# Combining a weight matrix as it is read, and reordering normalised rows for an unstrided transpose, in a scheduled attention + two-FFN kernel

## The chip, the cores and the metric

The kernel runs on one core of a Trainium2 chip. The engines named below are PE (TensorE, matrix products), PEld (its weight loads), DVE (VectorE), ACT (ScalarE), POOL (GpSimd) and SP (SyncE, whose queue issues all DMA transfers here). The metric is device time in microseconds (us) of one execution, lower is better.

## The reference

```python
# attention: two softmax attentions per head (4x downsampled, and a band of |i-j| < 4), added
out_up = np.repeat(sm_attn(q_d, k_d, v_d), factor, axis=2)
...
x = (out_up + out_local) -> (4, 576, 512)
# first feed-forward, gated
k = np.maximum(xk @ w_k, 0.0);  v = k * k @ w_v
x = v * sigmoid(xr @ w_r)
# second feed-forward
xn = (x - mu) / np.sqrt(var + 1e-06) * g_ln
ch = np.maximum(xn @ w_ch1, 0.0) @ w_ch2        # w_ch1 512 x 2048, w_ch2 2048 x 512
return x + ch
```

The weights come as float64, so a row of 512 elements is 4 KB. 2304 tokens are taken in six chunks of 384.

## The kernel before

**Products.** Every float32 factor is split in a high part (rounded to the format that PE multiplies, by a cast on ACT or DVE) and a low part (the difference, a subtraction on DVE or POOL); `mm3` (L793) makes one product of three matmuls.

**Weights.** `load_f32` (L399) reads 512 KB of float64 into a tile `w` (two of them) and makes float32 of it with two ACT operations (L411, L413) and two DVE operations (L418, L422), into a tile `wf` (two of them). `load_split` (L426) then splits it: a cast (L391 or L392) and a subtraction (L436).

**The second feed-forward** runs in three passes of two chunks each. Its first product uses a seven-product scheme of 2x2 blocks in all passes; w_ch1's seven combinations were prepared earlier (`w1_combine`) and lie in DRAM as `s_dram`, read back as tiles `sa`. In the first pass the second product is plain: `m2_h` makes the hidden values of step f (f = 0 to 7; the 16 row blocks of w_ch2 are used in pairs f and f+8), with DVE adding partial sums from PSUM (`u` L1129, `t` L1135 and L1138, `c` L1142 and L1146) and making low parts (`c11l`, `c22l`, `c12l`, `c21l`, L1115), and `m2_acc` multiplies them with the pair's high and low parts (`w20h` to `w215l`) into `pso`. In the second and third pass the second product too is made of seven, and needs w_ch2's combinations, which `w2_combine` (L1198) prepares during the first pass and writes to `t_dram`.

**`w2_combine` before.** For each pair f it puts the float32 rows together again by adding high and low part (L1215, two additions of 512 elements), then makes four differences of 256 elements in place (L907), splits each into a tile `t` (cast L391 or L392, subtraction L903) and writes the tile to DRAM (L1225). The tiles `t` live in four buffers that go by the tag `wa`; a fifth `t` must wait until the first one's write has landed. Each pair also writes copies of its parts (L1207). All eight pairs are released by `after`, a step of the first pass's products that lies three steps before the pair's own (parameter `tg`).

**Normalisation.** `m2_prep` (L972) normalises a chunk's rows (`x1t`, L1005, DVE), writes them to `z_dram` (L1008), reads them back 32 partitions at a time as `zb` (L1020), and transposes 32x32 blocks on DVE (L1026): feature 4p+kt goes to partition p, so the transpose reads every fourth element. The rows of w_ch1 and g_ln are read in the same order of features.

**Order of the work.** Nothing is issued in the order of the code. `add` collects operations with their dependences, a due time and a cost; `Plan.order` builds, for each engine, one fixed sequence, choosing between ACT, DVE and POOL where an operation has several ways; SP's queue too is one sequence. On the chip each engine works through its own sequence and waits where it must. So a late operation holds back all that stand behind it on its engine.

## Time and profile before

| | us |
|---|---|
| three runs | 766.68, 768.57, 770.2 |
| median | 768.57 |
| the profiled execution | 770.0 |
| its span in the trace | 767.9 |

The profiled execution lies 1.4 us above the median of the runs, and 2.1 us of it lie outside the traced span. Times in the rows below count from the start of the span. The first pass of the second feed-forward runs from about 388 to 523 us, the other two to 764.5 us.

### The profile page before, as it was taken

The numbers are of one execution on the slowest core, as the hardware profiler recorded it, in microseconds if no ns is written. First come the engines' busy times: TensorE is split into PE (matmuls) and PEld (weight loads), VectorE is DVE, ScalarE is ACT, GpSimd is POOL, SyncE is SP. The second block draws the span as 40 slices with busy tenths as digits, with TensorE's granted clock in tenths as the row PEclk, the third lists the DMA queues.
The fourth block names the chain that finished last, engine by engine and source line by source line (L and its number), as shares of the span: only waits on it lengthen the run. The fifth ranks groups of instructions, "written<-read, shape, count | busy, mean of one in ns | idle before, by whom it ended". The sixth has DMA issues, their size and how long they took to land.

```text
span 767.9 us, 17471 instructions
## 1 busy us (share of the span) xinstructions
PE 744.3 (97%) x6248; PEld 662.6 (86%) x6248; DVE 622.6 (81%) x1322; ACT 469.2 (61%) x1079; POOL 93.7 (12%) x143
## 2 busy tenths in 40 slices
PE   9899999999999999999999999889999999999998
PEld 6778777888778798888989888778999999999998
DVE  5889999998975958978996889698777996344986
ACT  5789998987885856858841444363346552443552
POOL 3002112212100000000010000140012112110101
PEclk9999999999999999999999999899999999999999
DMA  8998595887786996982388999789999888986684
GB/s 186 184 191 188 165 195 130 170 178 154 202 179 202 277 322 179 281 248 98 108 293 256 285 298 332 272 268 347 329 295 345 235 255 268 391 261 209 203 269 147
DMA packets 199325, 180.33 MB, mean 235 GB/s; under 512 B 92480, under 2 KB 139976, under 8 KB 199240
## 3 DMA queue, kind: packets, MB, share of 16 engines
q1 hardware_dynamic: 199240, 179.23, 80.3%
q8 instruction: 50, 0.82, 0.5%
q14 instruction: 35, 0.29, 0.1%
HBM read 134.09 MB, written 45.09 MB: 233 GB/s over the span
## 4 chain that ended last, share of the span: by engine, by line
PE 70%; DVE 12%; DMA 10%; ACT 5%; issue 3%; POOL 1%; SPq 0%; DVEq 0%; ACTq 0%; POOLq 0%
PE pso L796 6%; PE pso L794 6%; PE pso L795 6%; PE psh L794 6%; PE psh L795 6%; PE psh L796 6%; DMA w<-in_moe_w_ch_dram 4%; PE psk L794 4%; PE psv L794 4%; PE psv L795 4%; PE psv L796 4%; PE psk L796 3%; PE psk L795 3%; DMA sa<-s_dram 2%; PE sc L645 2%
## 5 line engine op out<-in xcount | busy, mean ns | idle before, releaser
L794 PE MATMUL psh<-xn,sa 128*128 128x384 f32 x336 | 114.6, 341 | 5.1 <-DVE c L1142 2.9
L795 PE MATMUL psh<-xn,sa 128*128 128x384 f32 x336 | 113.4, 337 | 0.0
L796 PE MATMUL psh<-xn,sa 128*128 128x384 f32 x336 | 113.2, 337 | 0.0
L391 ACT CAST hh<-q 128x384 fp32r<-128x384 f32 x109 | 56.2, 516 | 48.0 <-PE pso L795 43.7
L796 PE MATMUL pso<-ta,hl 128*128 128x256 f32 x300 | 84.4, 281 | 0.0
L794 PE MATMUL pso<-ta,hh 128*128 128x256 f32 x300 | 84.3, 281 | 0.0
L795 PE MATMUL pso<-ta,hh 128*128 128x256 f32 x300 | 84.3, 281 | 0.0
L794 PEld LDWEIGHTS psh<-xn,sa 128*128 128x128 f32 x336 | 63.4, 189 | 11.0 <-DVE c L1142 4.1
L795 PEld LDWEIGHTS psh<-xn,sa 128*128 128x128 f32 x336 | 63.4, 189 | 1.9
L796 PEld LDWEIGHTS psh<-xn,sa 128*128 128x128 f32 x336 | 63.4, 189 | 0.0
L903 DVE TENSOR_TENSOR hl<-q,hh 128x384 fp32r<-128x384 f32 x92 | 51.3, 564 | 9.2 <-ACT hh L391 8.5
L796 PEld LDWEIGHTS pso<-ta,hl 128*128 128x128 f32 x300 | 56.7, 189 | 0.0
L795 PEld LDWEIGHTS pso<-ta,hh 128*128 128x128 f32 x300 | 56.6, 189 | 0.0
L794 PEld LDWEIGHTS pso<-ta,hh 128*128 128x128 f32 x300 | 56.5, 188 | 0.0
L1273 ACT ACTIVATE q<-q 128x384 f32<-128x384 f32 x48 | 25.2, 525 | 45.3 <-DVE q L1263 26.3
L411 ACT ACTIVATE wf<-w 128x512 f32<-128x512 f32 x48 | 32.2, 672 | 20.3 <-DMA w<-in_moe_w_ch_dram 13.9
L418 DVE SCALAR_TENSOR_TENSOR wf<-wf,w 128x512 uint32<-128x512 uint32 x48 | 33.3, 695 | 10.5 <-ACT w L413 9.2
L903 POOL TENSOR_TENSOR hl<-q,hh 128x384 fp32r<-128x384 f32 x20 | 21.3, 1072 | 144.3 <-ACT hh L391 144.2
L395 ACT ACTIVATE kr<-psk 128x384 f32<-128x384 f32 x46 | 22.4, 487 | 26.1 <-PE psk L796 23.9
L859 DVE TENSOR_TENSOR kl<-kr,kh 128x384 fp32r<-128x384 f32 x43 | 23.8, 552 | 15.2 <-ACT kr L858 14.9
L907 DVE TENSOR_TENSOR q<-q,q 128x384 f32<-128x384 f32 x60 | 35.1, 592 | 0.0
L413 ACT ACTIVATE w<-w 128x512 uint32<-128x512 uint8 x52 | 34.8, 670 | 0.0
(593 smaller groups left out, 2109.1 us busy)
## 6 DMA issues: line engine op xcount, KB each, us to landing
sa<-s_dram SPq DMA_DIRECT2D x168, 256.0 KB, 4.9
ta<-t_dram SPq DMA_DIRECT2D x100, 256.0 KB, 3.5
w<-in_moe_w_ch_dram SPq DMA_DIRECT2D x32, 512.0 KB, 5.5
s_dram<-s SPq DMA_DIRECT2D x56, 256.0 KB, 4.0
t_dram<-t SPq DMA_DIRECT2D x32, 256.0 KB, 4.4
vw<-in_v_dram SPq DMA_DIRECT2D x62, 96.0 KB, 4.3
x_dram<-r SPq DMA_DIRECT2D x18, 256.0 KB, 2.7
x1t<-x_dram SPq DMA_DIRECT2D x6, 768.0 KB, 5.7
```

The costliest lines, as they stand in the source:

```text
L391: return [("ACT", c_act(n), lambda: nc.scalar.copy(dst(), src()), False), ("DVE", c_dve(n, True), lambda: nc.vector.tensor_copy(dst(), src ...
L395: return [("ACT", c_act(n, True), lambda: nc.scalar.activation(dst(), src(), AF.Relu), False), ("DVE", c_dve(n), lambda: nc.vector.tensor_ ...
L411: add("ACT", c_act(512), prio, lambda: nc.scalar.activation(f(), w64().bitcast(F32)[:, :, 1], AF.Abs, scale=2.0 ** -112), r=[w64], w=[f])
L413: add("ACT", c_act(512), prio, lambda: nc.scalar.activation(w64()[:, :, 0], w64().bitcast(U8).rearrange("p a (b c) -> p a b c", c=4)[:, :, ...
L418: lambda: nc.vector.scalar_tensor_tensor(fu(), fu(), 3, w64()[:, :, 0], op0=ALU.logical_shift_left, op1=ALU.bitwise_or),
L794: nc.tensor.matmul(ps, lh, rh, start=start, stop=False, skip_group_check=more)
L795: nc.tensor.matmul(ps, lh, rl, start=False, stop=False, skip_group_check=more)
L796: nc.tensor.matmul(ps, ll, rh, start=False, stop=stop, skip_group_check=more)
L859: add(either(C, lambda e: e.tensor_tensor(kl(), kr(), kh().bitcast(F32), op=ALU.subtract)), 0, prio, None, r=[kr, kh], w=[kl])
L903: add(either(n, lambda e: e.tensor_tensor(lo(), src(), hi().bitcast(F32), op=ALU.subtract)), 0, prio, None, r=r + wh, w=wl)
L907: add(either(n, lambda e: e.tensor_tensor(out(), a(), b(), op=op)), 0, prio, None, r=r, w=w)
L1273: return [("ACT", c_act(n), lambda: nc.scalar.activation(t(), t(), AF.Relu), False), ("DVE", c_dve(n, True), lambda: nc.vector.tensor_scal ...
```

## The change

Two edits, and a parameter of the planner:

1. For f = 2 to 7 the new `w2_pair` reads both row blocks of a pair, splits them, and gives the two float32 tiles to `w2_combine`, which makes its differences in them in place. The two additions (L1215 before) remain for f = 0 and 1 alone. These six pairs are no longer released by `after`; they are due ten microseconds (`tp`) after the pair's reading. Both blocks of a pair are due at the same time.
2. The normalisation (L1005 before) writes its 512 features in another order (4 x 4 x 32), so that the block for kt lies in 32 neighbouring elements and the transpose reads them unstrided. The rows of w_ch1 and g_ln are read in their natural order, 128 neighbouring rows instead of every fourth.
3. `ahead`, with which the planner lets SP's queue run ahead of its transfers, goes from 1 to 2 us.

```diff
-    late=330.0, ahead=1.0, tp=0.5, tps=0.05, keep=2, tg=-3, b11=6, ne=12, we=52.842, wes=25.704, wel=6.378,
+    late=330.0, ahead=2.0, tp=10, tp0=0.5, tps=0.05, keep=2, tg=-3, b11=6, tq=0, ne=12, we=52.842, wes=25.704, wel=6.378,
...
-    def w1_rows(d, fo):
-        return w_ch1.rearrange("(p k) f -> k p f", k=KT)[d, :, 512 * fo:512 * fo + 512]
...
-        load_f32(w1_rows(d, fo), f, prio)
+        load_f32(w_ch1[d * P:(d + 1) * P, 512 * fo:512 * fo + 512], f, prio)
...
-                    x1t()[:, TT], x1t()[:, t], mv()[:, t, 0:1], rstd()[:, t:t + 1], op0=ALU.subtract, op1=ALU.mult),
+                    x1t()[:, TT].rearrange("p (a k f) -> p k a f", k=KT, f=32),
+                    x1t()[:, t].rearrange("p (k a f) -> p k a f", k=KT, f=32),
+                    mv()[:, t, 0:1], rstd()[:, t:t + 1], op0=ALU.subtract, op1=ALU.mult),
...
-                        out=b()[:, q, C // 2 * h:C // 2 * h + C // 2], in_=zb()[:, :, kt:P:KT]),
+                        out=b()[:, q, C // 2 * h:C // 2 * h + C // 2], in_=zb()[:, :, 32 * kt:32 * kt + 32]),
...
+    def w2_pair(f, prios):
+
+        raw = []
+        for k in range(2):
+            g, prio = f + F4 * k, prios[k]
+            hi = Buf(wp, [P, 512], F32R, f"s{2 * f + k}h", 1, f"w2{g}h")
+            lo = Buf(wp, [P, 512], F32R, f"s{2 * f + k}l", 1, f"w2{g}l")
+            b = Buf(wk, [P, 512], F32, "wf", 2, "t")
+            load_f32(w_ch2[g * P:(g + 1) * P, :], b, prio)
+            split(512, hi, lo, b, prio, [b], [hi], [lo])
+            W2[g] = hi, lo
+            raw.append(b)
+        w2_combine(f, prios[1] + PRM["tp"], None, raw)
...
-        for k in range(2):
+        for k in range(0 if made else 2):
...
         for o in plan.ops[n0:]:
-            o.deps.add(after)
+            if after is not None:
+                o.deps.add(after)
...
+    if KEEP == 1:
+        for f in range(2, F4):
+            w2_pair(f, [T_2 + PRM["w2"] + PRM["w2s"] * (2 * f - 4)] * 2)
...
-            for f in range(F4):
-                w2_combine(f, T + DP * (PRM["tp"] - 1.0 + PRM["tps"] * f), acc_op[min(max(f + PRM["tg"], 0), F4 - 1)])
+            for f in range(2 if KEEP == 1 else F4):
+                w2_combine(f, T + DP * (PRM["tp0"] - 1.0 + PRM["tps"] * f), acc_op[min(max(f + PRM["tg"], 0), F4 - 1)])
```

What the planner makes of it, at three places. First DVE's sequence in step f = 5 of the first pass, where combinations stand between the partial sums. Before (`t` without a step's line L1138 is a combination; `c21l` and `u` are the step's own work):

```order
L903 TENSOR_TENSOR t<-t 128x256
L1215 TENSOR_TENSOR t<-w23h,w23l 128x512
L903 TENSOR_TENSOR t<-t 128x256
L907 TENSOR_TENSOR t<-t 128x256
L1215 TENSOR_TENSOR t<-w211h,w211l 128x512
L903 TENSOR_TENSOR t<-t 128x256
L907 TENSOR_TENSOR t<-t 128x256
L1115 SCALAR_TENSOR_TENSOR c21l<-c_6736,c21h 128x384
L1129 TENSOR_TENSOR u<-psh_6747,u 128x384
```

The same step's end in the changed kernel:

```order
L903 TENSOR_TENSOR t<-t 128x256
L1229 TENSOR_TENSOR t<-w20h,w20l 128x512
L1229 TENSOR_TENSOR t<-w28h,w28l 128x512
L907 TENSOR_TENSOR t<-t 128x256
L1114 SCALAR_TENSOR_TENSOR c12l<-c_6687,c12h 128x384
L1145 TENSOR_TENSOR c_6733<-psh_6654,u 128x384
L907 TENSOR_TENSOR t<-t 128x256
L388 COPY u<-psh_6714 128x384
L1114 SCALAR_TENSOR_TENSOR c21l<-c_6733,c21h 128x384
L903 TENSOR_TENSOR t<-t 128x256 x2
L1128 TENSOR_TENSOR u<-psh_6763,u 128x384
```

The pairs 2 to 5 are combined by then, and pair 0 follows directly on pair 6; one L903 stands ahead of `c21l` in these rows instead of three, and two now stand between `c21l` and `u`.

Second, DVE's sequence at the turn from the first feed-forward (`r` is its last output, L877) to the second. Before:

```order
L418 SCALAR_TENSOR_TENSOR wf<-wf,w_5565 128x512
L907 TENSOR_TENSOR raw_5428<-raw_5428 128x384
L422 SCALAR_TENSOR_TENSOR wf<-w_5565,wf 128x512
L877 TENSOR_TENSOR r<-psv_5388,r 128x512
L877 TENSOR_TENSOR r<-psv_5394,r 128x512
L877 TENSOR_TENSOR r<-psv_5400,r 128x512
L1129 TENSOR_TENSOR u<-psh_5663,u 128x384
L436 TENSOR_TENSOR w210l<-wf,w210h 128x512
```

In the changed kernel:

```order
L903 TENSOR_TENSOR w210l<-t,w210h 128x512
L903 TENSOR_TENSOR t<-t 128x256
L907 TENSOR_TENSOR t<-t 128x256
L1082 TENSOR_TENSOR xn<-raw_5428,xn 128x384
L907 TENSOR_TENSOR t<-t 128x256
L903 TENSOR_TENSOR t<-t 128x256
L907 TENSOR_TENSOR t<-t 128x256
L903 TENSOR_TENSOR t<-t 128x256
L877 TENSOR_TENSOR r<-psv_5388,r 128x512
L877 TENSOR_TENSOR r<-psv_5394,r 128x512
L877 TENSOR_TENSOR r<-psv_5400,r 128x512
L1128 TENSOR_TENSOR u<-psh_5662,u 128x384
```

Pair 2 is combined here, ahead of `r` and `u`; the conversion of its second block has moved further up.

Third, SP's queue at the same place (`w` are reads of w_ch2, `sa` the first product's weights of step 1). Before:

```order
L405 DMA w_5637<-in_moe_w_ch_dram 128x1024
L1094 DMA sa_5667<-s_dram 128x512
L1094 DMA sa_5677<-s_dram 128x512
L405 DMA w_5706<-in_moe_w_ch_dram 128x1024
L879 DMA x_dram<-r 128x512
L977 DMA x1t<-x_dram 128x3x512 x2
L879 DMA x_dram<-r 128x512
L1094 DMA sa_5779<-s_dram 128x512
```

In the changed kernel:

```order
L405 DMA w_5636<-in_moe_w_ch_dram 128x1024
L405 DMA w_5658<-in_moe_w_ch_dram 128x1024
L1093 DMA sa_5668<-s_dram 128x512
L1220 DMA t_dram<-w210h 128x2x256
L1093 DMA sa_5683<-s_dram 128x512
L1220 DMA t_dram<-w210l 128x2x256
L1239 DMA t_dram<-t 128x512 x3
L879 DMA x_dram<-r 128x512
L1239 DMA t_dram<-t 128x512
L1093 DMA sa_5744<-s_dram 128x512
```

The third `sa` of step 1 now stands behind the four writes of pair 2's combinations.

Counted over the kernel, DVE's sequence loses twelve additions L1215 and thirteen operations L907 on `t`, POOL's gains thirteen operations on `t` (9 before, 22 after), six copies of 256 elements (L1196) go from ACT to DVE, and PE's sequence holds the same matmuls, a few of them moved past each other in the first pass.

## Rows read from the trace of the kernel before

**Rows 1.** The page's first part: busy us (share of span) x instructions.

```profile
span 767.9 us, 17471 instructions
...
PE 744.3 (97%) x6248; PEld 662.6 (86%) x6248; DVE 622.6 (81%) x1322; ACT 469.2 (61%) x1079; POOL 93.7 (12%) x143
```

**Rows 2.** Busy time by stretch: length, then PE, PEld, DVE, ACT, POOL, granted clock, DMA.

```profile
388.00:425.00 37.00, 36.66 (x186) 33.21 (x185) 28.11 (x66) 10.70 (x24) 2.00 (x2) 1.00 0.85 274
425.00:455.00 30.00, 28.73 (x140) 24.88 (x139) 25.54 (x53) 14.95 (x28) 1.02 (x1) 1.00 0.94 301
455.00:482.00 27.00, 26.68 (x130) 22.93 (x129) 24.74 (x53) 12.77 (x27) 2.21 (x3) 1.00 0.98 322
482.00:500.00 18.00, 15.17 (x64) 13.35 (x64) 12.44 (x30) 5.67 (x14) 3.08 (x4) 0.81 0.76 267
500.00:523.00 23.00, 19.27 (x91) 15.97 (x90) 21.92 (x46) 14.87 (x40) 7.77 (x7) 1.00 0.81 271
```

**Rows 3.** PE's waits from 388 to 523: us in total, times, longest.

```profile
PE psh L794 <- DVE c L1142: 2.9, 2, 2.2
PE pso L796 <- DVE c21l L1115: 2.8, 1, 2.8
```

**Rows 4.** PE in order of time: start, us, operation, idle before it.

```profile
485.56 0.40 PE L795 MATMUL pso<-w213l,c21h 128*128 128x512 f32 x1
488.78 0.79 PE L796 MATMUL pso<-w213h,c21l 128*128 128x512 f32 x1 [2.83 <-DVE c21l L1115]
```

**Rows 5.** The stretch behind that wait, columns as in Rows 2.

```profile
488.70:494.80 6.10, 6.02 (x16) 5.07 (x17) 4.74 (x11) 1.32 (x4) 2.49 (x4) 0.50 0.63 233
```

**Rows 6.** DVE in order of time ahead of the same wait.

```profile
484.65 0.69 DVE L1215 TENSOR_TENSOR t<-w211h,w211l 128x512 f32<-128x512 f32 x1
487.50 0.43 DVE L903 TENSOR_TENSOR t<-t 128x256 fp32r<-128x256 f32 x1 [2.16 <-ACT t L391]
488.18 0.55 DVE L1115 SCALAR_TENSOR_TENSOR c21l<-c,c21h 128x384 fp32r<-128x384 f32 x1
```

**Rows 7.** ACT in order of time there.

```profile
487.06 0.41 ACT L391 CAST t<-t 128x256 fp32r<-128x256 f32 x1 [2.44 <-DMA t_dram<-t]
```

**Rows 8.** Instructions writing the tiles t, 455 to 522: ns min/median/max; DMA landing.

```profile
L907 DVE TENSOR_TENSOR t<-t x25: 411/419/1220, 462.2 to 517.4; 128x256 f32<-128x256 f32 x25
L907 POOL TENSOR_TENSOR t<-t x7: 726/736/892, 464.8 to 502.1; 128x256 f32<-128x256 f32 x7
...
DMA to landing us min/median/max: 3.6/4.4/5.1
```

**Rows 9.** The additions L1215 alone, 455 to 523: length, DVE busy (count), clock, DMA.

```profile
455.00:523.00 68.00, 11.34 (x16) 0.95 0.86 290
```

**Rows 10.** DVE's transposes, strided and unstrided, ns min/median/max.

```profile
L1026 DVE STREAM_TRANSPOSE raw<-zb x48: 473/492/541, 361.9 to 569.8; 128x192 f32<-128x192 f32 x48
...
L704 DVE STREAM_TRANSPOSE pT<-e x16: 530/570/574, 20.0 to 227.9; 128x384 f32<-128x384 f32 x16
```

**Rows 11.** The normalisation L1005, ns min/median/max.

```profile
L1005 DVE TENSOR_SCALAR x1t<-x1t,mv,rstd x18: 536/542/550, 324.9 to 554.2; 128x512 f32<-128x512 f32 x18
```

**Rows 12.** DVE operations that ran beside a POOL operation, in order of time.

```profile
492.39 1.04 DVE L1215 TENSOR_TENSOR t<-w212h,w212l 128x512 f32<-128x512 f32 x1
...
517.40 1.22 DVE L907 TENSOR_TENSOR t<-t 128x256 f32<-128x256 f32 x1
```

**Rows 13.** DVE in order of time at the turn to the second feed-forward.

```profile
387.58 2.00 DVE L877 TENSOR_TENSOR r<-psv,r 128x512 f32<-128x512 f32 x3
389.50 0.55 DVE L1129 TENSOR_TENSOR u<-psh,u 128x384 f32<-128x384 f32 x1
```

**Rows 14.** PE at the third product of step 1 (f = 1), in order of time.

```profile
400.11 0.33 PE L794 MATMUL psh<-xn,sa 128*128 128x384 f32 x1
```

**Rows 15.** The page's list of DMA issues: count, KB each, median us to landing.

```profile
sa<-s_dram SPq DMA_DIRECT2D x168, 256.0 KB, 4.9
```

**Rows 16.** PE's waits from 523 to 768: us in total, times, longest.

```profile
PE psh L794 <- DMA sa<-s_dram: 1.0, 2, 0.6
```

More of the change, by code (lines that the diff above doesn't have):

```diff
@@ L904, in split, with minus @@
             r=r + wh, w=wl)
-    def minus(n, out, a, b, prio, r, w, op=ALU.subtract):
-        add(either(n, lambda e: e.tensor_tensor(out(), a(), b(), op=op)), 0, prio, None, r=r, w=w)
+    def minus(n, out, a, b, prio, r, w, op=ALU.subtract, skip=False):
+        add(either(n, lambda e: e.tensor_tensor(out(), a(), b(), op=op))[skip:], 0, prio, None, r=r, w=w)
     n_put = [0, 0]
@@ L938, in w1_combine @@
             else:
-                load_f32(w1_rows(d, fo), a[x], prio)
+                load_f32(w_ch1[d * P:(d + 1) * P, 512 * fo:512 * fo + 512], a[x], prio)
         def put(i, src):
@@ L1196, in w2_stay, with w2_combine @@
             add(copy(256, B11[f][x], lambda x=x: W2[f][x]()[:, :256]), 0, prio, None, r=[W2[f][x]], w=[B11[f][x]])
-    def w2_combine(f, prio, after):
+    def w2_pair(f, prios):
[10 more added lines that the diff above has]
+        w2_combine(f, prios[1] + PRM["tp"], None, raw)
+    def w2_combine(f, prio, after, raw=None):
         n0 = len(plan.ops)
@@ L1210, in w2_combine @@
                     w=[(td, (i, f, x)) for i in range(i0, i0 + n)], lat=2.2)
-        raw = [Buf(wk, [P, 512], F32, "wf", 2, "t") if KEEP == 1 else
-               Buf(wk, [P, 512], F32, f"xr{HL[k]}", 1, "t") for k in range(2)]
-        for k in range(2):
+        made = raw is not None
+        raw = raw or [Buf(wk, [P, 512], F32, "wf", 2, "t") if KEEP == 1 else
+                      Buf(wk, [P, 512], F32, f"xr{HL[k]}", 1, "t") for k in range(2)]
+        for k in range(0 if made else 2):
             h_, l_ = W2[f + F4 * k]
             add(either(512, lambda e, k=k, h_=h_, l_=l_: e.tensor_tensor(
-                raw[k](), h_().bitcast(F32), l_().bitcast(F32), op=ALU.add)), 0, prio, None, r=[h_, l_],
+                raw[k](), h_().bitcast(F32), l_().bitcast(F32), op=ALU.add))[k < PRM["tq"] % 4:], 0, prio, None, r=[h_, l_],
                 w=[(raw[k], 0), (raw[k], 1)])
@@ L1220, in w2_combine @@
         for n, (o, x, y) in enumerate(((0, 1, 0), (1, 3, 1), (3, 3, 0), (2, 2, 3)), 3):
-            minus(256, s(o), s(x), s(y), prio, [rk(x), rk(y)], [rk(o)])
+            minus(256, s(o), s(x), s(y), prio, [rk(x), rk(y)], [rk(o)], skip=n - 3 < PRM["tq"] // 4 % 8)
             t = Buf(w1tiles, [P, 2, 256], F32R, "wa", 4, "t")
@@ L1408, in attn_moe_kernel @@
                     out=raw()[KT * i:KT * i + KT, :P],
-                    in_=src.rearrange("(p k) -> k p" if src is g_ln else "(k p) -> k p", p=P)), w=[(raw, i)], lat=2.2)
+                    in_=src.rearrange("(k p) -> k p", p=P)), w=[(raw, i)], lat=2.2)
             vps = Buf(ps_k, [P, 512], F32, "pk", 2, "vps")
@@ L1497, in attn_moe_kernel @@
         moe_x(c, pvs[c], rr, T + DU + 1 + PRM[f"rx{c}"])
+    if KEEP == 1:
+        for f in range(2, F4):
+            w2_pair(f, [T_2 + PRM["w2"] + PRM["w2s"] * (2 * f - 4)] * 2)
     for i, f in enumerate(w2_order[4:], 4):
-        W2[f] = load_split(w_ch2[f * P:(f + 1) * P, :], i, f"w2{f}", T_2 + PRM["w2"] + PRM["w2s"] * (i - 4))
+        if f not in W2:
+            W2[f] = load_split(w_ch2[f * P:(f + 1) * P, :], i, f"w2{f}", T_2 + PRM["w2"] + PRM["w2s"] * (i - 4))
     DP = PRM["dp"]
```

## The prediction

> **What bounds the kernel now.** I read the page first: PE is busy 744.3 of the span's 767.9 us [rows 1]. The change adds no matmul and takes none away, so it can only give back time in which PE waits or runs slowly, and what such time there is bounds the gain. The busy time by stretch shows where: over the first pass of the second feed-forward, which the change rearranges, PE is not busy for 0.34 + 1.27 + 0.32 us up to 482, and for 2.83 + 3.73 us from 482 to 523 [rows 2]. [...] The pool is 1.93 + 6.56 + 3.05 = 11.5 us, of which 9.6 lie behind 482. Behind the first pass PE's waits on named releasers come to the 1.0 us of one group [rows 16].
>
> The list of PE's waits names DVE for it: `c` L1142 and `c21l` [rows 3]. In order of time, the long one runs from 485.6 to 488.8 and ends on `c21l` [rows 4]. `c21l` had nothing late of its own: DVE stood for 2.16 us at a subtraction of a combination `t`, and the two rows behind it had to wait [rows 6]. That subtraction waited for ACT's cast, and the cast for a write to `t_dram` [rows 7]: the fifth `t` needs a buffer whose write takes 4.4 us to land [rows 8]. Right behind that wait the clock is at 0.50 [rows 5]. So the loss is a chain: combinations come faster than four buffers can be written, and DVE, in one sequence, holds the first product's sums behind them. From 500 on DVE is simply full, 21.92 of 23 us [rows 2].
>
> **The change, part by part.** *Additions removed.* Sixteen of L1215 take 11.34 us, 0.71 each [rows 9]; twelve go, 8.5 us of DVE. All the pairs stood in one stretch because `after` released them late; now six pairs are combined as they are read. Counted in the two sequences, behind `c21l` of step 5 (488 us) and its neighbours stood about five pairs of eight operations on `t` and ten L1215; now about two and a half pairs, two L1229, and pair 7's conversion (six operations of 512 elements, for which I take L1215's 0.71). With 0.42 us for an operation on `t` [rows 8], DVE's 12.44 + 21.92 = 34.4 us between 482 and 523 [rows 2] become 34.4 - 7.1 - 16.8 + 1.4 + 8.4 + 4.3 = 24.6, and with the six copies that come over from ACT (no such row; between nothing and 0.42 each, I take 0.42) 27.1. PE needs 41 - 9.6 = 31.4 us for what it does there. DVE is then no longer full, and the 3.73 us behind 500 should go. The stall at 485 needs both the crowd and the buffers; the crowd shrinks, but pair 0 follows directly on pair 6 and pair 1 on pair 7, eight `t` through four buffers each time. I keep one wait of the size seen, 2.2 us [rows 6], without a fall of the clock, as PE has more behind it. Its bounds are nothing and the whole 9.6.
>
> *POOL's share.* Thirteen operations on `t` go from DVE to POOL: DVE saves 13 x 0.42 = 5.4 us, POOL spends 13 x 0.74 = 9.6 [rows 8]. That is not free for DVE: beside a POOL operation, an addition took 1.04 instead of 0.71 and a difference 1.22 instead of 0.42 [rows 9, 12, 8], so 0.33 to 0.80 us more each, 4.3 to 10.4 us for thirteen. DVE's saving by the additions and this one together, 13.9 us, then falls to between 3.5 and 9.6. It remains a saving, in a stretch where it was full, so I leave the estimate above. [...]
>
> *The turn at 388.* Pair 2 is now combined ahead of `r` and `u`. Seven operations on `t` are 2.9 us of DVE; two conversions of 0.71 that stood there have gone further up. `r` starts at 387.58 and `u` ends at 390.05 [rows 13]; behind `u` PE waits for its bank. Bounds: nothing, if PE's last products are what `r` waits for, and 2.9. I take 1.0, under the net 1.5, as `r` does read PE's last results.
>
> *SP's queue.* The third `sa` of step 1 now stands behind pair 2's four writes. These are ready when their subtractions are, which stand ahead of `r`, so about 388 to 390; with 4.9 us to landing [rows 15] the `sa` is there at about 395, and PE wants it at 400.11 [rows 14]. Cost nothing, covered by step 0's products; without that cover it would cost up to the 4.9.
>
> *The reordered normalisation.* A transpose of 192 elements takes 492 ns strided; an unstrided one of 384 takes 570 [rows 10]. An unstrided one of 192 is not in the trace: it lies between half of 570 and the present 492, a saving of 0 to 0.21 us. I take 0.1, so 1.6 us of DVE in each pass's sixteen. L1005 writes the same 512 elements in another order; between no change and the 0.71 of L1215, that is 0 to 0.17 us on its 0.54 [rows 11, 9], for six in a pass up to 1.0. Both stand where DVE has room: it is busy 28.11 of 37 us in the stretch where the first pass has them, and PE loses 0.34 there [rows 2]. Zero in the sum, at most 1.6 either way (PE's 0.34 + 1.27). The natural order of w_ch1's and g_ln's rows moves the same bytes; PE's waits ahead of 388 name no transfer. Zero. `ahead` changes SP's sequence only, as counted.
>
> *Sum.* 9.6 - 2.2 - 1.0 = 6.4 us gained. From the profiled execution's own 770.0 that is 763.6; against the median, which lies 1.4 lower, 762.2, and I forecast **762**.
>
> **The rivals.** *The wait stays (no change).* Eight `t` in a row still meet four buffers, twice, and POOL's operations slow DVE; one of the two places pays what 482 to 495 paid, 2.83 + 3.05 = 5.9 us, while the 3.73 behind 500 goes: 3.73 - 1.0 = 2.7 gained, 765.9; were both to pay, about 768 to 770. For it: landing of 4.4 us, two times for eight tiles, is 8.8 us in a step of some 16 (388 to 523 in eight steps). Against it: reads and combinations of pairs 2 to 5 are gone from there. [...]
>
> *More than I count.* All waits of the first pass go, and the turn costs nothing: 768.6 - 11.5 = 757; with the 1.0 of the later passes, 756. For it: the early waits are DVE's as well, and DVE has less to do. Against: 425 to 455 now gets pairs 4 and 5 complete.
>
> *Slower.* The place is SP's single queue: each pair's four writes now stand between the `sa` of the next step, and a `t` that waits for its buffer holds back the `sa` behind its write. If each of the pairs 3 to 7 pays once what 482 to 495 paid, 5 x 5.9 = 29.5 us come in and 11.5 go, with 1.0 for the turn: 768.6 + 19 = 787.6. It makes the kernel measurably slower from about 3 us for each pair on ((11.5 + 3.8) / 5). For it: the DMA share is 0.94 and 0.98 from 425 to 482 already [rows 2], and the writes come earlier into that. Against it: in the first pass none of PE's waits is on an `sa`, though writes stood between them before as well.
>
> *It does not do what it says.* The transposes may be no faster; as they are hidden, the time is the forecast's.
>
> **How the numbers follow.** Forecast 0.54 (its own range 759 to 765), the wait stays 0.22, more 0.13, slower 0.11. The range reaches over the second and third case and leaves out the slower one and some of the edges: 756 to 769. The three runs lie within 3.5 us, so 0.5% (3.8 us) is about what a measurement here can tell from no change; that is 764.7 and 772.4. Faster: forecast and more, 0.67; within: 0.22; slower: 0.11.
>
> **What would show it.** Right: no L1215 for pairs 2 to 7 and DVE under about 90% between `c21l` of step 5 and the first pass's end; no wait of PE over 2.5 us there and no stretch at 0.50; `u` at the turn at most a microsecond later; transposes nearer 390 than 492 ns and L1005 near 542. Wrong: a wait of PE of 3 us or more on `c21l`, `c` or `u` with a cast on a `t_dram` write behind it (the wait stays); PE waiting on `sa` in the first pass (slower); all PE waits there under 2 us in sum (more). The forecast fails above all if waits move to the step where pair 0 follows pair 6.

## The result, and the profile after

The changed kernel takes 759.83 us (median of 6 runs, 756.88 to 764.1) against 769.68 (6 runs, 766.68 to 773.1): a ratio of 0.9868, 95% interval 0.9826 to 0.991. Run once more with its variants it came to 0.9871 (0.9842 to 0.9899). The forecast was 762 us, in a range of 756 to 769.

The busy time by stretch of the changed kernel, in the stretches of [rows 2] and in one more (length, then PE, PEld, DVE, ACT, POOL, granted clock, DMA share, GB/s):

```profile
388.00:425.00 37.00, 36.16 (x178) 31.31 (x178) 30.05 (x70) 12.53 (x29) 5.83 (x7) 1.00 0.97 336
425.00:455.00 30.00, 29.52 (x143) 25.50 (x143) 25.74 (x57) 15.13 (x30) 4.83 (x5) 1.00 0.83 256
455.00:482.00 27.00, 27.00 (x136) 24.29 (x135) 23.65 (x47) 14.17 (x31) 7.30 (x9) 1.00 1.03 360
482.00:500.00 18.00, 18.00 (x91) 16.12 (x90) 15.52 (x35) 9.44 (x24) 4.21 (x5) 1.00 0.99 347
500.00:523.00 23.00, 22.95 (x120) 21.02 (x119) 18.03 (x39) 10.39 (x25) 5.55 (x5) 1.00 0.97 340
523.00:640.00 117.00, 114.74 (x812) 113.23 (x811) 94.26 (x203) 54.00 (x113) 15.25 (x14) 1.00 0.88 272
```

The last of these stretches in the kernel before:

```profile
523.00:640.00 117.00, 116.05 (x802) 114.28 (x801) 98.50 (x209) 57.81 (x124) 16.62 (x15) 1.00 0.91 299
```

Read the difference of length and PE. From 482 to 523 PE is busy for all but 0.05 us, where 6.56 us were missing, and the clock is at 1.00 throughout, where half of the 6.10 us at 0.50 [rows 5], 3.05 us, is counted as lost: 9.56 us come back. From 388 to 482, 0.84 + 0.48 us are missing instead of 1.93: 0.61 more. From 523 to 640, 2.26 us are missing instead of 0.95: 1.31 are given back. The sum is 8.86 us; the spans are 767.9 and 759.0, 8.9 apart.

What the clock of 0.50 cost is to be seen in the starts of PE's matmuls in the kernel before, two pairs of them at 0.50 and two behind it at 1.00:

```profile
490.37 0.52 PE L794 MATMUL psh<-xn,sa 128*128 128x384 f32 x1
490.69 0.52 PE L795 MATMUL psh<-xn,sa 128*128 128x384 f32 x1
...
492.61 0.63 PE L794 MATMUL pso<-w213h,c21h 128*128 128x512 f32 x1
493.04 0.63 PE L795 MATMUL pso<-w213l,c21h 128*128 128x512 f32 x1
...
496.68 0.33 PE L794 MATMUL psh<-xn,sa 128*128 128x384 f32 x1
496.85 0.33 PE L795 MATMUL psh<-xn,sa 128*128 128x384 f32 x1
...
499.28 0.40 PE L794 MATMUL pso<-w26h,c11h 128*128 128x512 f32 x1
499.51 0.39 PE L795 MATMUL pso<-w26l,c11h 128*128 128x512 f32 x1
```

At 0.50 the next matmul starts 0.32 us (384 elements) or 0.43 us (512) later, at 1.00 0.17 or 0.23. The sixteen from 488.78 on, ten of 512 and six of 384, take 6.33 us up to the start of the next; at the spacings of 1.00 that is an estimated 3.4, so 3.0 us were lost there, beside the 3.05 counted.

PE's waits in the changed kernel, first from 388 to 523 (where the kernel before has those of [rows 3]), then from 530 to 600 (us in total, times, longest):

```profile
PE psh L794 <- DVE c L1145: 0.5, 1, 0.5
PE psh L794 <- ACT u L387: 0.3, 1, 0.3
PE pso L796 <- DVE c11l L1114: 0.2, 1, 0.2
PE psh L794 <- DVE t L1134: 0.2, 1, 0.2
...
PE psh L794 <- ACT q L1288: 1.5, 1, 1.5
PE psh L794 <- DVE q L1275: 0.6, 1, 0.6
```

None of the first pass is on `c21l` any more. The waits of the second pass are new. DVE in order of time shows where they come from: four transposes stand ahead of a sum, and wait for a read `zb`:

```profile
549.94 1.16 DVE L1025 STREAM_TRANSPOSE raw<-zb 128x192 f32<-128x192 f32 x4 [1.78 <-DMA zb<-z_dram]
551.02 0.52 DVE L1275 TENSOR_TENSOR q<-psh,u 128x384 f32<-128x384 f32 x1
...
555.44 1.16 DVE L1025 STREAM_TRANSPOSE raw<-zb 128x192 f32<-128x192 f32 x4 [1.92 <-DMA zb<-z_dram]
556.52 0.52 DVE L1284 TENSOR_TENSOR q<-psh,u 128x384 f32<-128x384 f32 x1
```

Next the operations of [rows 10, 11] and the turn of [rows 13] in the changed kernel (ns min/median/max; then start and us):

```profile
L1025 DVE STREAM_TRANSPOSE raw<-zb x48: 334/338/380, 361.9 to 560.1; 128x192 f32<-128x192 f32 x48
...
L1002 DVE TENSOR_SCALAR x1t<-x1t,mv,rstd x18: 531/541/548, 325.2 to 540.8; 128x512 f32<-128x512 f32 x18
...
387.75 1.88 DVE L877 TENSOR_TENSOR r<-psv,r 128x512 f32<-128x512 f32 x3
389.55 0.54 DVE L1128 TENSOR_TENSOR u<-psh,u 128x384 f32<-128x384 f32 x1
```

A transpose takes 338 ns instead of 492, the normalisation 541 instead of 542, and `u` ends at 390.09 instead of 390.05.

### The profile page after: what moved, and what is told of

Read it like the earlier page. It is cut to its first block, busy times and chain, and to the rows that moved or that the text cites. A ratio compares the mean times of both kernels' runs of the same rounds, so it can differ in the third digit from the quotient of the medians.

```text
span 759.0 us, 17473 instructions
## 1 busy us (share of the span) xinstructions
PE 741.1 (98%) x6248; PEld 659.9 (87%) x6248; DVE 609.6 (80%) x1304; ACT 466.5 (61%) x1073; POOL 101.2 (13%) x155
## 4 chain that ended last, share of the span: by engine, by line
PE 73%; DMA 10%; DVE 8%; ACT 6%; issue 2%; SPq 0%; POOL 0%; DVEq 0%; POOLq 0%; ACTq 0%
PE pso L796 8%; PE pso L795 8%; PE pso L794 8%; PE psh L794 6%; PE psh L795 6%; PE psh L796 6%; PE psk L794 4%; PE psk L796 3%; PE psk L795 3%; DMA zb<-z_dram 3%; PE psv L794 3%; PE psv L796 3%; PE psv L795 3%; DMA w<-in_moe_w_k_dram 2%; PE warm L449 1%
## 5 line engine op out<-in xcount | busy, mean ns | idle before, releaser
L903 DVE TENSOR_TENSOR hl<-q,hh 128x384 fp32r<-128x384 f32 x93 | 51.4, 557 | 9.6 <-ACT hh L391 8.5
L794 PEld LDWEIGHTS pso<-ta,hh 128*128 128x128 f32 x300 | 56.5, 188 | 0.0
L903 POOL TENSOR_TENSOR hl<-q,hh 128x384 fp32r<-128x384 f32 x19 | 19.8, 1047 | 152.8 <-ACT hh L391 152.7
L907 DVE TENSOR_TENSOR q<-q,q 128x384 f32<-128x384 f32 x60 | 34.2, 577 | 0.0
L411 ACT ACTIVATE wf<-w 128x512 f32<-128x512 f32 x36 | 24.2, 672 | 16.1 <-DMA w<-in_moe_w_k_dram 5.3
L818 DVE SCALAR_TENSOR_TENSOR tmu<-xT,oms,tmu 128x384 f32<-128x384 f32 (+1 forms) x64 | 31.8, 513 | 2.7 <-ACT tmu L812 2.6
```

The costliest lines, as they stand in the source:

```text
L411: add("ACT", c_act(512), prio, lambda: nc.scalar.activation(f(), w64().bitcast(F32)[:, :, 1], AF.Abs, scale=2.0 ** -112), r=[w64], w=[f])
L794: nc.tensor.matmul(ps, lh, rh, start=start, stop=False, skip_group_check=more)
L818: lambda t=t, o=o, n=n, prv=prv, kt=kt: nc.vector.scalar_tensor_tensor(t()[:, o:o + n], prv(), om[:, kt:kt + 1], t()[:, o:o + n], op0=ALU. ...
L903: add(either(n, lambda e: e.tensor_tensor(lo(), src(), hi().bitcast(F32), op=ALU.subtract)), 0, prio, None, r=r + wh, w=wl)
L907: add(either(n, lambda e: e.tensor_tensor(out(), a(), b(), op=op))[skip:], 0, prio, None, r=r, w=w)
```

## The experiments

Executions differ by up to 2.8 us in when the second feed-forward begins (zb_lat6 left out), and 2.4 us of that are there 70 us after the start, where all kernels still have the same sequences (the matmul `psk<-xkh,wk00h` there begins at 67.81 us in late_act_copy, at 70.17 in early_adds). So beside the ratio of the times, the table gives, from the profiled execution, the us from the start of the last matmul of the first feed-forward (`psv<-wv7h,kl`) to the span's end. That column rests on one execution of each kernel. The one of the kernel before took 770.0 us, where its later runs have medians of 767.7 to 767.9; late_both's is the fastest of its seven, early_adds' the slowest of its five. So differences of 2 us in it say little.

| kernel | ratio, 95% interval | that start | span | from start to end |
|---|---|---|---|---|
| before | 1 | 388.47 | 767.9 | 379.4 |
| changed | 0.9868 (0.9826-0.991) | 388.51 | 759.0 | 370.5 |
| after_again | 0.9871 (0.9842-0.9899) | 387.37 | 757.8 | 370.4 |
| pairs_strided | 0.9893 (0.9865-0.9921) | 387.77 | 757.7 | 369.9 |
| unstrided_late | 0.9962 (0.9942-0.9981) | 387.21 | 764.3 | 377.1 |
| ahead1 | 0.9929 (0.9903-0.9954) | 389.50 | 761.0 | 371.5 |
| early_adds | 0.9936 (0.9913-0.9958) | 389.72 | 762.6 | 372.9 |
| late_act_copy | 1.0024 (1.0002-1.0046) | 386.92 | 765.4 | 378.5 |
| late_seven | 0.9985 (0.9963-1.0008) | 386.90 | 764.0 | 377.1 |
| late_both | 0.9975 (0.9954-0.9996) | 387.06 | 761.5 | 374.4 |
| stalls | 0.9964 (0.9947-0.998) | 388.18 | 762.8 | 374.6 |
| t_on_dve | 0.9954 (0.9933-0.9975) | 387.60 | 763.8 | 376.2 |
| zb_lat4 | 0.989 (0.987-0.9911) | 388.25 | 759.1 | 370.9 |
| zb_lat6 | 0.996 (0.9939-0.9981) | 384.28 | 759.7 | 375.4 |

In zb_lat6 work has moved past that start (in zb_lat4 a little), so their last column says less. The results of ahead1, late_seven, t_on_dve, zb_lat4 and zb_lat6 come from sequences that were planned anew, so not only the named edit differs.

**Each edit alone.** after_again is the changed kernel. pairs_strided takes edit 2 out of it, unstrided_late puts edit 2 alone into the kernel before; the diffs are those of the change.

> The changed kernel once more, beside its variants on the same chip. Both theories expect 0.983 to 0.991 of the kernel before, no wait of PE over 1 us from 388 to 523, and no stretch at a granted clock of 0.50 there.

> The changed kernel with the normalisation, the transposes and the rows of w_ch1 and g_ln as before (strided transposes); every engine's sequence is that of the changed kernel. Theory: the gain is the pairs' earlier combining, and the transposes are hidden, so the 48 transposes cost DVE 48 x (0.492 - 0.338) = 7.4 us more and the kernel stays within 2 us of the changed one (0.985 to 0.990 of before). Rival: the transposes stand on the path, in the second pass above all, where PE waits for values that DVE makes behind them; then 2.5 us (16 of them) to 7.4 us come back, 0.990 to 0.997.

> The kernel before with the reordered normalisation and unstrided transposes alone; every engine's sequence is that of before. Theory: the wait of about 2.8 us on c21l at 485, the sixteen matmuls at 0.50 behind it and the wait of about 2.2 us on c near 517 are all still there, and the time is within 0.4% of before (767 to 772 of a before of 769.7). Rival: the transposes carry part of the gain, 2.5 to 7.4 us, 0.990 to 0.997.

after_again repeats the time, but not every expectation: PE waits 1.2 us on `c` L1145 and 1.0 us on `c` L1141, at 428 and 445, though all sequences are those of the changed kernel. Its clock stays at 1.00, and from 455 to 523 it loses 0.06 us. pairs_strided keeps the gain: its interval overlaps that of after_again, and from start to end it is 0.5 us shorter. Edit 2 alone saves 2.9 us by the medians (0.9962, interval 1.5 to 4.5 us). That is the edge of the theory's 0.4% and lies inside the rival's range, so this run does not separate them; nor does it separate the transposes from the new order in which the rows of w_ch1 and g_ln are read. PE's waits of unstrided_late from 386 to 530:

```profile
PE pso L796 <- DVE c21l L1117: 2.6, 1, 2.6
PE psh L794 <- DVE c L1144: 2.2, 1, 2.2
```

The two long waits of [rows 3] stand as before. What has gone are waits of 0.50 and 0.77 us on `c`, which ended at 427.7 and 443.5, in and behind the stretch (420 to 435) where sixteen of the transposes stand. The clock does not explain the saving: it comes back sooner behind the first wait, after some 3.0 us instead of 6.3, but falls a second time, behind the wait on `c` (below). With the pairs moved as well, nothing of the saving is to be seen any more.

**The planner's `ahead`.** The edit is `ahead=2.0` to `ahead=1.0` in the changed kernel.

> The changed kernel planned with ahead = 1 as before (sequences are planned anew, so a few operations stand elsewhere). Theory: the pairs' combining carries the gain whatever ahead is, 0.983 to 0.992. Rival: SP's longer run ahead is what gets the early pairs' reads and writes through in time; then half of the gain or more is lost, 0.993 to 1.0, with waits of PE on c21l, c or sa in the first pass. To be seen beside it: whether the new waits of the second pass (0.6 and 1.55 us, behind transposes that wait for zb) come with ahead = 2; if so they are gone here.

Neither cleanly: nearly half of the gain is lost by the times, of which the trace places 1.1 us behind the start (waits of 1.6 us on `t` L1137 and 1.1 on `c` in the first pass, while the second pass loses less: its waits on `q` are gone, as the expectation asked to see). The rest lies ahead of it, where all sequences are those of the changed kernel but for SP's from 384 on, so it is not explained.

**Place or saving.** early_adds does the twelve additions again, at the new place; late_act_copy takes all sixteen off DVE, at the old place:

```diff
+            if made and n in (3, 5):
+                first = lambda k=n // 5, h_=h_, l_=l_: nc.vector.tensor_tensor(
+                    raw[k](), h_().bitcast(F32), l_().bitcast(F32), op=ALU.add)
```

```diff
-            add(either(512, lambda e, k=k, h_=h_, l_=l_: e.tensor_tensor(
-                raw[k](), h_().bitcast(F32), l_().bitcast(F32), op=ALU.add)), 0, prio, None, r=[h_, l_],
+            add(either(512, lambda e, k=k, h_=h_, l_=l_: nc.scalar.copy(
+                raw[k](), h_().bitcast(F32))), 0, prio, None, r=[h_, l_],
```

> The changed kernel with the twelve additions put back: each of pairs 2 to 7 makes its two float32 rows once more from high and low part, on DVE, right before its differences, at the changed kernel's place; all other instructions and their sequences are those of the changed kernel. DVE has 12 x 0.69 = 8.3 us more to do. Theory (place): what helped is that the pairs left the crowd behind 455, so most of the gain stays, 0.985 to 0.992 of before, with no wait of PE over 2 us and no stretch at 0.50. Rival (saving): DVE's 8.3 us were the gain; 0.994 or more.

> The kernel before with its sixteen additions taken off DVE: in their place stands a copy of the high part alone on ACT (the low part is left out of the combinations), so DVE loses all 11 us of additions, and the combining stays where it was. Theory (place): the wait on c21l near 485 stays at 2 to 3 us, with a cast behind a write to t_dram at its root, and the clock falls behind it; the waits at 500 and 517, where DVE was full, go: 0.993 to 0.998. Rival (saving): all these waits go, 0.984 to 0.990.

With the additions kept, half of the gain remains by the times and 6.5 of 9.0 us by the trace; no wait in the first pass is over 1.6 us and the clock stays at 1.00. So both theories hold a part there. At the old place the saving, moved to ACT, gives nothing at all: 1.0024 lies outside both expected ranges. The run is not the saving alone, since ACT has sixteen copies of 0.61 to 0.62 us more, and DVE waits 7.1 us for its casts between 455 and 523, where it was 2.9. Busy time of late_act_copy, then ACT and DVE in order of time at its long wait:

```profile
482.00:500.00 18.00, 13.91 (x55) 11.65 (x54) 9.78 (x23) 6.71 (x17) 3.93 (x5) 0.81 0.71 254
500.00:523.00 23.00, 19.73 (x98) 17.26 (x97) 18.39 (x37) 17.38 (x46) 7.27 (x7) 1.00 0.82 272
...
484.25 0.41 ACT L391 CAST t<-t 128x256 fp32r<-128x256 f32 x1 [2.19 <-DMA t_dram<-t]
...
484.69 0.43 DVE L903 TENSOR_TENSOR t<-t 128x256 fp32r<-128x256 f32 x1 [3.54 <-ACT t L391]
485.03 0.42 DVE L907 TENSOR_TENSOR t<-t 128x256 f32<-128x256 f32 x1
485.37 0.55 DVE L1115 SCALAR_TENSOR_TENSOR c21l<-c,c21h 128x384 fp32r<-128x384 f32 x1
```

DVE is busy 9.78 of 18 us and PE still loses 4.09 us. What DVE no longer adds it waits for at the next `t`: 3.54 us behind a write to `t_dram`, with `c21l` behind it. From 500 to 523 PE still loses 3.27 us, though DVE is busy for 18.39 of 23 us only; so what made it wait is not a DVE that is full from end to end. In the wait itself, 2.37 us on `c` up to 517.34, DVE has no pause: four operations on `t` and a `c22l` stand ahead of `c`, and two of the four, at 513.64 and 514.80, take 1.24 and 1.21 us instead of 0.42, beside POOL. The kernel before has the same at its wait on `c` up to 519.95, where the operations of 1.04 and 1.22 us stand.

**The buffers.** late_seven gives the combinations three more tiles; late_both is that and late_act_copy's edit.

```diff
-            t = Buf(w1tiles, [P, 2, 256], F32R, "wa", 4, "t")
+            k = n_put[1] % 7
+            n_put[1] += 1
+            t = Buf(w1tiles, [P, 2, 256], F32R, *(("wa", 4) if k < 4 else (f"alt{k - 4}", 1)), "t")
```

> The kernel before with seven buffers for the combinations instead of four (three tiles that are idle in the first pass take part); additions and release as before, sequences planned anew. Theory (four buffers at the root of the long wait): the wait of 2.8 us on c21l and the stretch at 0.50 behind it go, the waits where DVE is full stay, 0.990 to 0.995. Rival (DVE's work is the limit): the wait stays or moves, 0.997 to 1.003.

> The kernel before with both cures at once: seven buffers for the combinations, and the additions taken off DVE (a copy of the high part on ACT in their place, the low part left out of the combinations); the combining stays late. All sequences but DVE's and ACT's are those of the kernel with seven buffers. Each cure alone gave at most 0.15%. Theory (two limits lie on each other, the buffers' writes and DVE's load): together they give most of what the change gave, 0.985 to 0.991 of before, with under 3 us of PE's waits from 450 to 523 and no stretch at 0.50. Rival (what counts is that reads and combinations come earlier, a third thing): 0.995 or more.

With seven buffers the time is the rival's (0.9985): the wait on `c21l` shrinks to 0.6 us, and DVE is busy for 18.00 of 18 us from 482 to 500; PE then waits 2.7 us on `c12l`, 12 us later. With both cures the time falls by 0.25%, the rival's too; the trace, 5.0 us shorter from start to end, still has a long wait. DVE in order of time there, in late_both, and PE's matmul that waits:

```profile
492.17 0.55 DVE L1142 TENSOR_TENSOR c<-psh,u 128x384 f32<-128x384 f32 x1
492.63 0.41 DVE L903 TENSOR_TENSOR t<-t 128x256 fp32r<-128x256 f32 x1
492.97 0.42 DVE L907 TENSOR_TENSOR t<-t 128x256 f32<-128x256 f32 x1
493.30 0.41 DVE L903 TENSOR_TENSOR t<-t 128x256 fp32r<-128x256 f32 x1
493.88 0.42 DVE L903 TENSOR_TENSOR t<-t 128x256 fp32r<-128x256 f32 x1 [0.16 <-ACT t L391]
494.40 0.43 DVE L907 TENSOR_TENSOR t<-t 128x256 f32<-128x256 f32 x1
495.30 0.43 DVE L903 TENSOR_TENSOR t<-t 128x256 fp32r<-128x256 f32 x1 [0.47 <-ACT t L391]
495.64 0.42 DVE L907 TENSOR_TENSOR t<-t 128x256 f32<-128x256 f32 x1
495.98 0.55 DVE L1115 SCALAR_TENSOR_TENSOR c22l<-t,c22h 128x384 fp32r<-128x384 f32 x1
496.44 1.08 DVE L1115 SCALAR_TENSOR_TENSOR c12l<-c,c12h 128x384 fp32r<-128x384 f32 x1
...
497.58 0.50 PE L796 MATMUL pso<-w26h,c12l 128*128 128x512 f32 x1 [2.46 <-DVE c12l L1115]
```

`c` is there at 492.7, `c12l` begins at 496.44: seven operations on `t` stand between them in DVE's fixed sequence, and two of these wait for ACT besides; `c12l` itself takes 1.08 us instead of 0.55, beside POOL. While the combining stays late, something of it stands ahead of a sum at the long waits seen here, and by the times the next limit eats most of what each cure takes away: late combining with less work on DVE, more buffers or both gave at most 0.25% (interval up to 0.46%); early combining with all its additions gave 0.64% (0.42 to 0.87%). By the single traces the two are nearer, 5.0 us for late_both and 6.5 for early_adds. That the place is worth more than the cures together rests on the times; by how much stays open.

**POOL's share.** In the changed kernel the differences and subtractions of `t` are planned for DVE alone.

```diff
-            minus(256, s(o), s(x), s(y), prio, [rk(x), rk(y)], [rk(o)], skip=n - 3 < PRM["tq"] // 4 % 8)
+            add([("DVE", c_dve(256), ..., True)], 0, prio, None, r=[rk(x), rk(y)], w=[rk(o)])
```

> The changed kernel with the differences and subtractions of the combinations allowed on DVE alone, none on POOL (planned anew). DVE has some 22 operations of 0.42 us more, 9.2 us, and none of these stands beside POOL any more. Theory: DVE has room for them now, and what POOL took over was worth little, so 0.985 to 0.991 of before. Rival: POOL's share is needed, 0.992 or more, with waits of PE on c and c11l in the first pass that grow.

The rival, by the time: two thirds of the gain go. PE waits 1.9 us at the turn (0.3 in the changed kernel) and 3.4 us in three waits on `c` L1141. But the run is no price for the thirteen operations that the change gave to POOL. It takes off all 22, of which the kernel before had nine on POOL as well. And at the turn DVE does the same operations in the same order as in the changed kernel, up to `u`; what differs is POOL, and with it the length of three of them. POOL and then DVE in t_on_dve:

```profile
381.58 4.89 POOL L1082 TENSOR_TENSOR xn<-raw,xn 128x384 fp32r<-128x384 f32 x3 [33.30 <-ACT xn L391]
...
382.94 1.51 DVE L903 TENSOR_TENSOR w210l<-t,w210h 128x512 fp32r<-128x512 f32 x1
384.37 1.23 DVE L1241 TENSOR_TENSOR t<-t 128x256 fp32r<-128x256 f32 x1
385.52 1.23 DVE L1236 TENSOR_TENSOR t<-t 128x256 f32<-128x256 f32 x1
```

In the changed kernel POOL makes one `xn` there and then waits until 388.23 for its subtraction of pair 2; the three operations take 0.68, 1.18 and 0.41 us. Without that subtraction POOL goes on with two more `xn`, and DVE's three operations take 1.7 us longer in sum. Pair 2's casts on ACT wait for them, and ACT's `u`, for which PE waits, stands behind those casts. So the 1.9 us are POOL's other work running beside DVE, and not more work on DVE.

**The new waits.** zb_lat4 and zb_lat6 plan the changed kernel with another latency of `zb`:

```diff
-                        w=[(zb, a)], lat=2.2)
+                        w=[(zb, a)], lat=4.2)
```

> The changed kernel, planned with 4.2 us instead of 2.2 as the time that a transfer zb takes beyond its queue (the trace shows 3.9 from issue to landing), so that DVE's transposes stand later in its sequence, behind the sums that PE waits for. Theory: the new waits of the second pass (2.5 us near 551 and 556, behind transposes that wait for zb) go, and the kernel is 1 to 2 us faster than the changed one, 0.983 to 0.987 of before. Rival: the transfers sa behind them, or the values made from raw, are late instead, and it stays at 0.986 to 0.990.

> The same with 6.2 us. Theory as for 4.2, 0.982 to 0.987; rival: transposes so late that the second pass starts without their values, 0.988 or more.

By the times both rivals: at 4.2 the same time, with 1.6 us on `t` at 505 and 1.3 on `sa` at 556 in place of those that went; at 6.2 a wait of 4.0 us on `t` L1134 at 391. No kernel tried beats the changed one.

**The clock.** stalls holds DVE up in two steps of the changed kernel by writing `c21l` repeatedly:

```diff
+            for _ in range(1 + more):
                 nc.vector.scalar_tensor_tensor(
...
+        res[1, 0] = h_split(c21, [c21], at_(6), "k2", "c21", {3: 5, 5: 9}.get(f, 0))
```

> The changed kernel with DVE held up twice: in the first pass the subtraction that writes c21l is done six times in step 3 (2.75 us more) and ten times in step 5 (5 us more), each time into the same tile. If a wait of PE of two to three us is by itself what lets its clock fall (theory), matmuls behind the two waits run at a granted clock of 0.50 for 2 to 6 us each, and the time is 0.994 to 1.005 of before. Rival: the fall in the kernel before needs more than the wait; behind one or both waits the clock stays at 1.0, and the time is 0.990 to 0.996.

Busy time around the longest wait and behind it, in stalls, in late_act_copy and in zb_lat6, and last behind the second long wait of unstrided_late:

```profile
484.00:486.90 2.90, 0.00 (x0) 0.00 (x0) 2.80 (x6) 0.47 (x1) 0.00 (x0) 1.00 0.00 0
486.90:488.00 1.10, 1.07 (x6) 1.08 (x7) 0.43 (x1) 1.10 (x4) 0.00 (x0) 1.00 0.98 361
```

```profile
482.90:486.00 3.10, 0.03 (x1) 0.03 (x1) 1.31 (x4) 0.81 (x2) 0.38 (x1) 0.87 0.98 369
486.00:488.00 2.00, 2.00 (x6) 1.82 (x7) 1.76 (x5) 0.93 (x2) 0.51 (x1) 0.50 0.64 236
...
391.60:395.60 4.00, 0.02 (x1) 0.00 (x1) 3.95 (x10) 2.46 (x7) 0.00 (x0) 1.00 0.97 317
395.60:396.60 1.00, 1.00 (x3) 1.00 (x4) 0.95 (x3) 1.00 (x3) 0.00 (x0) 0.50 0.98 158
...
517.00:519.00 2.00, 2.00 (x6) 1.61 (x5) 1.55 (x4) 1.77 (x4) 0.29 (x1) 0.50 0.83 251
```

In stalls one wait became 2.97 us long, the other only 1.43, and the clock stayed at 1.00 behind both. Waits of 2.46 (late_both), 2.62 (unstrided_late), 2.66 (late_seven), 2.83 (before), 3.09 (late_act_copy) and 3.98 us (zb_lat6) were followed by 0.50. The second wait of unstrided_late, 2.16 us on `c` up to 515.28, was followed by 0.50 as well, but the 2.16 us of the kernel before and the 2.37 us of late_act_copy, on the same `c`, were not. The theory falls: the length of the wait alone does not decide. By the time alone (0.9964) it would have stood.

## Why the prediction was right, by its steps

**The bound.** That only PE's lost time in the first pass could be won, and most of it behind 482, held: 9.56 us come from behind 482 and 0.61 from ahead of it, and 1.31 are given back later. after_again repeats the part behind 482 and not the 0.61: from 388 to 482 it loses 2.57 us, more than the 1.93 of the kernel before. The pool's 3.05 us take it that work at 0.50 needs half the time at 1.00, which no run shows; the spacing of the matmuls shows 3.0 us lost in their place.

**Additions removed, and one wait kept.** The sum kept one wait of 2.2 us. It did not come: nothing is lost from 455 to 500, and 0.05 us from 500 to 523. This is the largest mis-sized term, 2.2 predicted, 0.05 measured, and the reason that 6.4 us were forecast and 8.9 (trace) to 9.9 (medians) came. That the clock would hold behind such a wait "as PE has more behind it" was the author's assumption; no run shows this reason. That pair 0 follows directly on pair 6 cost PE nothing. The turn's 1.0 us did not come either, and the 1.31 us given back later were not foreseen; that these partly cancel, and 762 lies only 2.2 us from 759.83, is luck.

DVE was foreseen to be no longer full. Its share, 15.52 + 18.03 of 41 us, 82%, is under the 90% named, but the load is not the one of the sum: 27.1 us were forecast and 33.55 came, because the changed kernel, by then up to 10 us ahead, already has work of the later passes in that stretch, which the sum left out. Over nearly the same work of PE, from the first product `pso` of step 5 to the end of the first pass, it reads, in the kernel before, the changed one, early_adds and late_act_copy:

```profile
473.30:540.20 66.90, 60.12 (x286) 52.83 (x285) 56.25 (x124) 30.89 (x76) 14.03 (x15) 0.95 0.88 302
477.00:529.80 52.80, 52.75 (x267) 47.67 (x266) 43.05 (x97) 24.64 (x59) 13.06 (x14) 1.00 0.98 338
481.40:535.10 53.70, 53.42 (x268) 47.48 (x267) 45.27 (x102) 25.08 (x59) 13.36 (x14) 1.00 0.99 337
470.70:537.50 66.80, 59.44 (x284) 52.70 (x284) 49.17 (x112) 36.26 (x87) 12.96 (x14) 0.95 0.86 301
```

In the kernel before some 3 of PE's 60.1 us are lost at 0.50 (by the spacing of its matmuls), so DVE's 56.25 are nearly all of the 57 that PE needs; in the changed kernel they are 43.05 of 52.75. To that extent the forecast holds. But room is not enough. late_act_copy, at the old place, has DVE at 49.2 of the 56.5 us that PE needs, 87%, and PE loses 7.4 us in waits and some 3 at 0.50 (an estimate by the same spacings, for its 6 us at 0.50 from 486 to 492). early_adds, at the new place, has it at 45.3 of 53.4, 85%, and PE loses 0.3; what its additions cost lies mostly ahead, 4.1 us from 388 to 482, where the changed kernel loses 1.3.

So the reason given was only half right. The chain of writes, cast, subtraction and `c21l` was the cause of the wait at 485, since seven buffers took it from 2.8 to 0.6 us. But "from 500 on DVE is simply full", and with it the expectation that fewer additions free the 3.73 us there, failed: without any addition on DVE 3.27 us stayed (late_act_copy, with its copies on ACT). What the runs show in its place is the position of the combinations: in one fixed sequence they stand ahead of the sums, whether by their load, their waits for ACT or their waits for writes. By early_adds the new place is worth half to seven tenths of the gain, and at that place the removed additions are worth the rest; at the old place, moved to ACT, they were worth nothing. The place is the whole new plan here, with POOL's larger share in it; no run moves the combinations and leaves the rest of the plan as it was.

**The turn at 388.** 1.0 us was taken, nothing came: PE's wait on `u` is 0.3 us as before, though DVE does pair 2 ahead of `r`. It fits barely. Two runs in which DVE's work of pair 2 ends later paid at once: 1.6 us with its two additions done again (early_adds), 1.9 us where POOL ran beside it for longer (t_on_dve). In both the wait is on ACT's `u`, behind casts of pair 2.

**POOL's share.** It was kept out of the sum as a saving that might be eaten up. The thirteen operations are eight differences (L907) and five subtractions (L903); the change's description calls all of them L907. Their price on DVE was set too high. An estimate from the timelines, 375 us to the end of the first pass, takes DVE's operations with two inputs in SBUF that ran over 0.15 us longer than the median of their shape: eight of them, 4.9 us in all, before, and sixteen, 7.2 us, in the changed kernel. That is 2.4 us more, where the prediction had 4.3 to 10.4. What the thirteen are worth no run shows: t_on_dve (0.9954 against 0.9871) takes off nine more, and part of its loss is POOL's other work.

**SP's queue.** Nothing, as forecast. PE waits for no `sa` in the first pass, although the writes took a median of 5.5 us to land there instead of 4.4 [rows 8]. The slower rival needed these waits and did not come.

**The reordered normalisation.** Mechanism and bounds held: 0.154 us saved on each transpose (0 to 0.21; 0.1 taken), nothing on the normalisation. "Hidden, zero" holds within the changed kernel (pairs_strided). Alone it is 2.9 us by the times, with an interval from 1.5 us on, so probably above the 1.6 us named as the most.

**Between the passes.** A loss the prediction did not look for: 1.31 us more in the second pass, where a sum on DVE stands behind transposes that wait for `zb`. It is the mechanism of `c21l` over again, with another transfer at its root. after_again has the 1.5 us again; pairs_strided, with the same sequences, has 0.4 on `q` and 0.8 on an `sa` instead, so the sequences alone do not fix it.

**Of the rivals**, "more than I count" (756 to 757) came nearest in the first pass, and the second pass took back a part. "The wait stays" is excluded by the interval's upper end, 0.991.

## What to carry to other kernels

When several engines work through fixed sequences, look at what stands ahead of a late value, and try moving it away before making it cheaper: here the place was worth half of the gain or more, and the saving counted only at the new place. Test a suspected limit by lifting it alone, expect the next one right behind it, and check what the test itself adds elsewhere (copies on ACT, other work on POOL). Give work without a deadline to the time when its data come in, and look at the places where the plan is tight (a turn between stages) and at every instruction that waits for a transfer with an urgent one queued behind it. Compare traces from a common event onward, since starts can differ by more than some of the effects (2.8 us here), and do not trust one trace for the last 2 us (one of the kernel before lies 2.1 us or more above the later medians).

## What was not expected of the hardware

**The clock.** In the second feed-forward seven waits of PE, of 2.16 to 3.98 us, were followed by 0.50, and three, of 2.16, 2.37 and 2.97 us, by 1.00. The DMA share does not part them either: it was 0.00 in the 2.97 us of stalls, but 0.87 and 0.77 in the two others that kept 1.00, and 0.78 in the one of 2.16 us that lost it (0.96 to 1.06 in the other six). What decides stays open. How long 0.50 lasts differs too: sixteen matmuls in the kernel before [rows 5], about eight behind each of the two waits in unstrided_late.

**DVE beside POOL.** Rows of the changed kernel, POOL and then DVE, at three places (start, us):

```profile
463.24 0.75 POOL L903 TENSOR_TENSOR t<-t 128x256 fp32r<-128x256 f32 x1 [0.58 <-ACT t L391]
461.76 0.90 POOL L907 TENSOR_TENSOR t<-t 128x256 f32<-128x256 f32 x1 [1.72 <-DVE t L907]
...
463.36 1.05 DVE L1114 SCALAR_TENSOR_TENSOR c21l<-c,c21h 128x384 fp32r<-128x384 f32 x1
461.51 0.55 DVE L1114 SCALAR_TENSOR_TENSOR c12l<-c,c12h 128x384 fp32r<-128x384 f32 x1
462.17 0.56 DVE L1145 TENSOR_TENSOR c<-psh,u 128x384 f32<-128x384 f32 x1
```

Behind a POOL operation that began first, the subtraction took 1.05 us instead of 0.55 and ended 0.42 us after POOL did; where DVE began first it kept its 0.55, and POOL's difference took 0.90 us, where its shortest there took 0.74. A sum that reads one operand from PSUM kept its 0.56 beside POOL. Of DVE's 29 operations of the changed kernel that read PSUM beside POOL, from 375 to 530 us, none ran over 0.15 us longer than its like. From 388 to 523 PE of the changed kernel is not busy for 1.4 us in all, though DVE lost 7.2 us beside POOL by the estimate above. At the turn of t_on_dve (1.7 us in sum) and at the waits on `c` near 517 in the kernel before (1.04 and 1.22 us) and late_act_copy (1.24 and 1.21) operations lengthened beside POOL stood ahead of a value that PE waited for. What makes them longer no run shows.

**The strided transpose.** Reading every fourth float32 costs (492 - 338) / 192 = 0.80 ns for each of the 192 elements in a partition. The two kernels with one edit alone agree: 487 ns strided (pairs_strided), 337 unstrided (unstrided_late). What makes such a step cost that, no run shows.
